# Decode attention over a long cache: jumps back announced in all passes but the last, and a new order of the closing work

## The chip, the cores and the metric

One core of a Trainium2 chip. Its engines work side by side (their busy shares are in the table below): PE multiplies matrices, DVE and ACT work on vectors, SP starts the transfers, which 16 DMA engines carry. The metric is the device time of one execution in microseconds, median of several. A profile was taken of one execution of each kernel; its span is about 2 us shorter than the time of the same execution (2523.2 of 2525.35 us before).

## The reference, cut to what matters

```python
x = A_x; xn = _layernorm(x)                       # 1 x 1 x 448
q = (xn @ wq).reshape(1, 1, 16, 256)              # 16 heads, Dh = 256
scores = einsum("bhqd,bhkd->bhqk", q, k_cache) * Dh**-0.5     # 65536 keys per head
o = einsum("bhqk,bhkd->bhqd", softmax(scores), v_cache)
s = o.reshape(1, 1, 4096) @ wo
g = _silu(_silu(xn @ w1) @ w2)
return x + s * g
```

K and V caches are 537 MB each in bf16. Everything else is small.

## The kernel before: the parts that matter here

The caches are cut into 64 blocks of 8 MB for each of K and V (block i, counted from 0: head i // 4, a quarter of the keys). Three buffers `R[0..2]` of 8 MB take K block i, whose products with the query are summed by DVE (19 of 32 columns) and ACT (13 of 32), and then V block i, which PE multiplies with the exponentials. SP starts the loads. Each engine has its own loop of three blocks a pass, DVE and ACT with 21 passes and PE with 20; the rest is written out behind the loops.

```python
def load_k(i, s): take(sp, vf[s]); sp.dma_start(out=R[s], in_=block(Kd, i)).then_inc(kl[s], 16); ...
def load_v(i, s): take(sp, kf[s]); sp.dma_start(out=R[s], in_=block(Vd, i)).then_inc(vl[s], 16)

def pe_block(i, s):
    pe_turn()       # turn (transpose) O, the result of an earlier block: 8 small products
    pe_max(i)       # transpose row maxima, next query, broadcast the maximum
    pe_v(s)         # 64 products 128x512 with a V block; then vf[s] is free

def loop(e, a, b, step, **kw):
    return nc.Fori(a, b, step, engines={e}, head_slot={e: 0}, **kw)

with loop(ET.DVE, 0, LAST - 2, NR, hint_back_edge=True) as i: ...          # LAST = 63, NR = 3
with loop(ET.Activation, 0, LAST - 2, NR, hint_back_edge=True) as i: ...
with loop(ET.PE, 1, LAST - 4, NR, hint_back_edge=True) as i: ...
pe_block(NBLK - 3, 0)     # block 61: its PE work includes the products with V block 60
pe_turn(); pe_v(1)        # V block 61
pe_max(NBLK - 2)
...
# SP: K 63 in two halves once V 60 is used (vf[0]); V 62 in 4 parts; V 63 keys 0..64 in 2 parts;
#     first 2 parts of wo; V 63 keys 64..128 in 4 parts; last 2 parts of wo
# PE, closing:
keys(psO, 2, 2, vn, nl, 0, 3, True); pe_rows()                 # V 62
keys(psO, 2, 2, vn, nl, 3, 4, False, od); pe_bcast()
...
keys(psO2, 0, 1, vz, zl, 0, 2, True, od); pe_turn()            # V 63, keys 0..64
project(*pieces[0]); pe_rows(); project(h0, h0 + 3); pe_bcast(); project(h0 + 3, h1)
t15 = pe_sums(...)
keys(psO, 0, 1, vz, zl, 2, 3, True); pe_turn()                 # keys 64..96
keys(psO, 0, 1, vz, zl, 3, len(vz), False, od)                 # keys 96..128
project(*pieces[2]); pe_turn(); project(...)                   # the end
```

`hint_back_edge=True` puts, at the head of every pass, an instruction that announces the jump back at the end of the pass.

## Time and profile before

| what | before | how to read it |
|---|---|---|
| time | 2526.43 us (2525.76 to 2526.54, 3 runs) | median and range |
| span of the profiled run | 2523.2 us | its time was 2525.35 |
| busy: DVE, ACT, PE | 89%, 57%, 47% | shares of the span |
| DMA queue that loads the caches | 99.5% of 16 engines' span | the limit |
| from the row maxima of block 61 to the end | 104.6 us | see below |

The last line is a measure I use throughout: from the start of DVE's row-maximum reduction for K block 61 (2418.61 us, about where the loops end) to the end of the span. I call it the **closing stretch**. It is good to 0.1 us, as the span is printed. (The texts before the experiments call that block 62, counted from one.)

### The profile page before, as it was taken

What the parts mean: (1) busy time and instruction counts of PE and PEld (TensorE: products, weight loads), DVE (VectorE), ACT (ScalarE), POOL (GpSimd) and SP (SyncE); (2) the same over time, 40 slices, a digit from 0 to 9 for tenths busy, and PEclk for the clock granted to TensorE, in tenths of its full rate; (3) what the DMA queues carried; (4) which work ended last, traced back from release to release, by engine and by line L of the source; (5) the groups of instructions that cost most, each with busy time, mean ns of one, the idle gap of its engine ahead of it and who ended that gap; (6) DMA issues with size and microseconds to landing.
All of it is one profiled execution on the core that took longest, in us unless ns stands there. A gap on an engine that the chain in (4) does not pass through costs nothing. (4 is left out here: it accounts for less than half of the span.)

```text
span 2523.2 us, 29918 instructions
## 1 busy us (share of the span) xinstructions
PE 1198.1 (47%) x5125; PEld 500.5 (20%) x5125; DVE 2233.7 (89%) x10281; ACT 1443.9 (57%) x6992; POOL 2.5 (0%) x13
## 2 busy tenths in 40 slices
PE   3353543534535435445354354454553543534556
PEld 2121211212212112112121121221221211212222
DVE  6989889889899898898898988988989889889886
ACT  3656556556555565565565655655656556556554
POOL 0000000000000000000000000000000000000000
PEclk7676767767767767677676676676766767767778
DMA  9999999999999999999999999999999999999998
GB/s 423 417 430 433 434 431 433 433 432 432 432 432 432 433 434 437 434 435 433 433 433 432 432 432 432 432 433 434 439 434 433 433 433 433 432 432 432 432 412 346
DMA packets 22728, 1084.52 MB, mean 430 GB/s; under 512 B 2354, under 2 KB 4532, under 8 KB 4916
## 3 DMA queue, kind: packets, MB, share of 16 engines
q1 hardware_dynamic: 22706, 1084.30, 99.5%
q8 instruction: 6, 0.10, 0.0%
q14 instruction: 14, 0.11, 0.0%
q10 hardware_dynamic: 2, 0.00, 0.0%
HBM read 1084.29 MB, written 0.00 MB: 430 GB/s over the span
## 5 line engine op out<-in xcount | busy, mean ns | idle before, releaser
L271 ACT ACTIVATE R<-R 128x256 bf16<-128x256 bf16 x3328 | 1330.7, 401 | 697.1 <-ACTq L154 697.1
L249 DVE CUSTOM_DVE_ANT_0 R<-R,qcur 128x256 bf16<-128x256 bf16 x4864 | 1700.2, 417 | 0.0
L318 PE MATMUL bank<-R,PV 128*2 128x512 bf16 x4096 | 1023.7, 416 | 32.4 <-DMA R<-in_A_v_cache_dram 15.3
L238 DVE TENSOR_TENSOR R<-R,qcur 128x3328 bf16<-128x3328 bf16 x256 | 482.6, 1885 | 198.7 <-DVEq L154 198.6
L271 ACT ACTIVATION_READ_ACCUMULATOR R<-R 128x1 f32 x3328 | 620.2, 186 | 2.6 <-issue 2.6
L330 PE MATMUL bank<-ident,rmax 128*1 128x128 bf16 x65 | 17.1, 263 | 1021.6 <-PEq L154 1021.6
L318 PEld LDWEIGHTS bank<-R,PV 128*2 128x2 bf16 x4096 | 365.0, 90 | 663.1 <-issue 208.0
L249 DVE DVE_READ_ACCUMULATOR2_ANT S<- 128x1 f32 x4864 | 383.5, 79 | 0.0
L346 PE MATMUL bank<-eye,O 2*128 2x1 f32 x536 | 98.0, 300 | 236.8 <-PEq L154 236.8
L330 PEld LDWEIGHTS bank<-ident,rmax 128*1 128x1 bf16 x65 | 5.2, 79 | 1026.1 <-issue 1025.9
L346 PEld LDWEIGHTS bank<-eye,O 2*128 2x128 f32 x536 | 94.2, 257 | 254.8 <-issue 254.8
L284 ACT ACTIVATE hist<-bank 128x1 f32 (+1 forms) x65 | 11.1, 171 | 203.4 <-ACTq L154 203.4
L305 ACT COPY hist<-bank 128x2 f32 (+1 forms) x66 | 10.5, 160 | 120.0 <-ACTq L154 120.0
L214 DVE TENSOR_REDUCE gmax<-bank 1x1 bf16<-1x128 f32 x65 | 18.2, 281 | 36.2 <-DVEq L154 36.2
L231 DVE CAST qcur<-bank 128x256 bf16<-128x256 f32 x64 | 27.2, 425 | 20.2 <-DVEq L154 18.3
L297 ACT COPY O<-bank 2x512 f32<-2x512 f32 x67 | 37.5, 559 | 9.1 <-ACTq L154 9.1
L286 ACT ACTIVATE PV<-S,hist 128x128 bf16<-128x128 f32 (+1 forms) x65 | 26.0, 400 | 13.4 <-ACTq L154 13.1
L358 PE MATMUL bank<-q,ident 16*128 16x256 bf16 x63 | 24.4, 387 | 0.0
L224 DVE COPY S<-S 128x128 f32<-128x128 f32 (+1 forms) x65 | 14.7, 226 | 9.5
L225 DVE TENSOR_REDUCE rmax<-S 128x1 bf16<-128x128 f32 (+1 forms) x65 | 18.2, 279 | 0.0
L336 PE MATMUL bank<-gmax,ones_row 1*128 1x1 bf16 x65 | 10.3, 158 | 15.9 <-PEq L154 15.9
L336 PEld LDWEIGHTS bank<-gmax,ones_row 1*128 1x128 bf16 x65 | 6.5, 99 | 33.3 <-issue 33.3
(65 smaller groups left out, 101.7 us busy)
## 6 DMA issues: line engine op xcount, KB each, us to landing
R<-in_A_k_cache_dram SPq DMA_DIRECT2D x4, 4096.0 KB, 23.4
R<-in_A_v_cache_dram SPq DMA_DIRECT2D x7, 2048.0 KB, 23.1
R<-in_A_wq_dram SPq DMA_DIRECT2D x1, 3072.0 KB, 12.7
R<-in_A_wo_dram SPq DMA_DIRECT2D x2, 1120.0 KB, 17.5
R<-in_B_w_dram SPq DMA_DIRECT2D x1, 1568.0 KB, 27.2
R<-in_B_w_dram SPq DMA_DIRECT2D x1, 1344.0 KB, 5.8
R<-in_A_v_cache_dram SPq DMA_DIRECT2D x1, 1024.0 KB, 15.8
R<-in_A_v_cache_dram SPq DMA_DIRECT2D x2, 512.0 KB, 17.0
```

The costliest lines, as they stand in the source:

```text
L214: dve.reduce_max(out=gmax[0:1, :], in_=ps_m[0:1, :], axis=AX.X).then_inc(gm, 1)
L225: dve.reduce_max(out=rmax[:, :], in_=S[:, c0:c1], axis=AX.X).then_inc(rm, 1)
L231: dve.tensor_copy(out=qcur[:, :], in_=ps_q).then_inc(sd, 1)
L238: m = dve.tensor_tensor(out=pair, in0=pair, in1=qcur[:, None, :].to_broadcast([P, NA, Dh]), op=ALU.mult,)
L249: ins = dve.tensor_tensor_reduce(out=Kv[:, c, :], in0=Kv[:, c, :], in1=qcur[:, :], scale=1.0, scalar=0.0, op0=ALU.mult, op1=ALU.add, accum ...
L271: ins = act.activation(out=prod, in_=prod, func=ACT.Identity, accum_out=S[:, c : c + 1],)
L286: act.activation(out=PV[s][:, c0:c1], in_=S2[:, c0:c1], func=ACT.Exp, bias=col(0, 1), scale=scale, accum_out=col(1, 2),).then_inc(pv, 1)
L297: act.copy(out=O[:, :], in_=po).then_inc(oc, 1)
L318: ins = pe.matmul(po, lhsT=PV[t][:, c : c + 2], rhs=R[s][:, c * Dh : (c + 2) * Dh], start=(start and c == k0), stop=(stop and c == k1 - 2),)
L330: pe.matmul(ps_m[0:1, :], lhsT=rmax[:, 0:1], rhs=ident[:, :], start=True, stop=True).then_inc(tm, 1)
L346: ins = pe.matmul(ps_t[:, a : a + 1], lhsT=Ov[:, j, a, :], rhs=eye2[:, j : j + 1], start=(j == 0), stop=(j == 1),)
L358: pe.matmul(ps_q, lhsT=ident[0:H, at(h)].to_broadcast([H, P]), rhs=q16[:, :], start=True, stop=True,).then_inc(qr, 1)
```

## The change

Its intent: let the engines leave their loops without a stall, and use the time won by an order of the closing work in which the row maxima are turned early and the last V block comes in smaller parts.

```diff
-    def loop(e, a, b, step, **kw):
-        return nc.Fori(a, b, step, engines={e}, head_slot={e: 0}, **kw)
+    @contextmanager
+    def loop(g, a, b, step):                       # (set-up of register, names, alignment cut)
+        with nc.body(head, valid_engines=es):
+            g.br_eq(r, b - step, on_true=body, on_false=ann)      # last pass: announce nothing
+        with nc.body(ann, valid_engines=es):
+            hint = g.mark_branch_hint_location()
+            nc.br(body, engines=es)
+        with nc.body(body, valid_engines=es):
+            yield nc.snap(r, min_val=a, max_val=b - step)
+            nc.regs_alu(r, r, step, op=mybir.AluOpType.add)
+            g.br_lt(r, b, on_true=head, on_false=tail).branch_hint(hint)
-    vz = cuts(0, 32, 64, 96, 112, 120, 128)
+    vz = cuts(0, 32, 64, 80, 96, 112, 120, 128)
-        keys(psO, 2, 2, vn, nl, 0, 3, True)
+        keys(psO, 2, 2, vn, nl, 0, 2, True)
         pe_rows()
-        keys(psO, 2, 2, vn, nl, 3, 4, False, od)
+        keys(psO, 2, 2, vn, nl, 2, 3, False)
         pe_bcast()
+        keys(psO, 2, 2, vn, nl, 3, 4, False, od)
 ...
-        keys(psO2, 0, 1, vz, zl, 0, 2, True, od)
+        keys(psO2, 0, 1, vz, zl, 0, 1, True)
         pe_turn()
+        pe_rows()
+        keys(psO2, 0, 1, vz, zl, 1, 2, False, od)
+        pe_bcast()
         project(*pieces[0])
-        pe_rows(); project(h0, h0 + 3); pe_bcast(); project(h0 + 3, h1)
         t15 = pe_sums(ps_m[:, 0:NL], N1, NENT)
-        keys(psO, 0, 1, vz, zl, 2, 3, True)
         pe_turn()
-        keys(psO, 0, 1, vz, zl, 3, len(vz), False, od)
-        project(*pieces[2])
+        project(*pieces[1])
+        keys(psO, 0, 1, vz, zl, 2, len(vz), True, od)
+        project(h0, h0 + 2)
         t = pe_turn(tok=True)
+        project(h0 + 2, h1)
```

(Waits, ACT's and DVE's lines and moves within a line are cut.)

## The prediction

> **What bounds the kernel now.** I read the page first, then the chain that ended last, then stretches of the end, then the time order of single engines. The page's slices and its queue table say that the transfers are the limit for nearly all of the span:

> ```profile
> span 2523.2 us, 29918 instructions
> DMA  9999999999999999999999999999999999999998
> GB/s 423 417 430 433 434 431 433 433 432 432 432 432 432 433 434 437 434 435 433 433 433 432 432 432 432 432 433 434 439 434 433 433 433 433 432 432 432 432 412 346
> q1 hardware_dynamic: 22706, 1084.30, 99.5%
> ```

> The reader is to see 432 to 434 GB/s in slice after slice, and less only in the first two and the last two. One slice is 63 us. 1084.30 MB at 432.5 GB/s take 2507 us of the 2523: at most 16 us can be had without moving fewer bytes, and they sit at the ends. So this change, which moves no bytes, can gain only single microseconds of 2526, and the verdict of a 2% test (50 us) is all but settled. What is worth predicting is where those few microseconds go.

> The table of stretches near the end shows one hole in the stream (the last two columns are the DMA share and GB/s):

> ```profile
> 2380.00:2420.00 40.00, 19.94 (x79) 8.24 (x79) 35.40 (x163) 22.46 (x109) 0.00 (x0) 0.67 1.02 441
> 2420.00:2440.00 20.00, 14.31 (x55) 4.96 (x55) 16.73 (x78) 11.26 (x55) 0.00 (x0) 0.72 0.99 424
> 2440.00:2460.00 20.00, 18.34 (x91) 7.86 (x89) 17.75 (x83) 11.71 (x56) 0.00 (x0) 1.00 0.84 348
> ```

> PE in order of time shows its cause: three products of the first V block after PE's loop, then a stall, then the other 61.

> ```profile
> 2420.18 1.44 PE L318 MATMUL bank<-R,PV 128*2 128x512 bf16 x3
> 2427.17 15.35 PE L318 MATMUL bank<-R,PV 128*2 128x512 bf16 x61 [5.55 <-issue]
> 2442.35 0.17 PE L368 MATMUL bank<-ident 128*1 128x1 bf16 x1
> ```

> "issue" means that nothing in the profile held the engine: it had no instruction. The last K block may be loaded only when that V block has been used, so its load leaves SP at 2442.65, when the queue has run dry. DVE shows the same at its own exit: the query is in PSUM at 2458.62, the copy of it starts 7 us later.

> ```profile
> 2458.56 0.28 DVE L214 TENSOR_REDUCE gmax<-bank 1x1 bf16<-1x128 f32 x1 [0.94 <-DVEq L154]
> 2465.61 0.42 DVE L231 CAST qcur<-bank 128x256 bf16<-128x256 f32 x1 [6.77 <-DVEq L154]
> ```

> The DMA records of the trace agree: between 109 and 2424 us there is no instruction fetch at all, then a 16 KB one starts at 2424.64 (PE goes on at 2427.17) and an 8 KB one at 2463.76 (DVE goes on at 2465.61). In the last 16 us PE is the bound, without a pause:

> ```profile
> 2507.47 3.61 PE L318 MATMUL bank<-R,PV 128*2 128x512 bf16 x16 [0.99 <-DMA R<-in_A_v_cache_dram]
> 2511.01 1.10 PE L346 MATMUL bank<-eye,O 2*128 2x1 f32 x8
> 2512.04 3.61 PE L318 MATMUL bank<-R,PV 128*2 128x512 bf16 x16
> 2515.49 1.68 PE L662 MATMUL bank<-R,OT 128*1 128x448 bf16 x8
> 2517.10 1.10 PE L346 MATMUL bank<-eye,O 2*128 2x1 f32 x8
> 2518.13 1.01 PE L662 MATMUL bank<-R,OT 128*1 128x448 bf16 x4
> ```

> [...]a jump was announced and not taken. [...]granted clock 0.66 in 2460 to 2480, which holds a 9 us wait of PE, and 1.00 where it is busy.

> **The change part by part.** *The loops.* They run the same passes (21, 21 and 20) of the same bodies. Each pass gets a compare-and-branch and two short jumps: [...]none of it on the path, since the DVE has 11% of the span idle. In the last pass nothing is announced, so the block behind the loop should be fetched in time. That removes 5.55 us from PE and about 6.8 us from DVE.

> What PE's part is worth: V blocks in mid-loop take 15.3 to 16.4 us, so this one would end near 2436.5, not 2442.35, and the load of the last K block would leave 6 us earlier, before the queue is dry. The hole, 348 instead of 432 GB/s over 20 us, is (432-348)/432 x 20 = 3.9 us; by the byte records of 2436 to 2446 alone 2.7 us. But a transfer has landed only with its slowest DMA engine. In the landing records the last block before the hole reaches most of the 16 engines at 2441.6 to 2442.1, the laggard at 2443.5, and the hole lets the laggard catch up. So later landings come 0 to 2.7 us earlier; I take 1.3.

> What DVE's part is worth: its last block starts near 2458.8 instead of 2465.61. PE idles before the V block that precedes it and begins it with a cold clock, so I give back 0.5 us: 6.3 us earlier. The second half's row maxima, which PE turns at 2503.67 now, are then ready at about 2497.3.

> *The closing order.* From there PE is the path in the new order, with durations by start-to-start from the rows above: 16 products 3.45, a turn 1.03, a product of the projection 0.2. From 2497.3: row maxima 0.05; V keys 32 to 64, 3.45 (2500.8); broadcast 0.1; ten projection products 2.0 (2502.9); sums 0.36 (2503.3); turn 1.03 (2504.3); ten projection products 2.0 (2506.3); 32 products for keys 64 to 128, 6.9 (2513.2); four of the projection 0.8 (2514.0); turn 1.03 (2515.0); the last eight with the DVE's step behind them 1.8 (2516.8). After PE's last product the kernel now needs 2523.2 - 2519.14 = 4.06 us (two DVE operations and the store): 2520.9.

> Transfers needed on that way, by the landing records of before: V keys to 96 at 2507.4, to 112 at 2510.0, to 120 at 2511.3, to 128 at 2512.6, third part of wo at 2514.75, fourth at 2515.9. Less 1.3 each they are just in time, but for the third part of wo: 2513.45 against 2513.2. That adds 0.3. Splitting keys 64 to 96 in two lets PE begin before the whole has landed; it saves a wait, no work. Sum: 2521.2, with 0.1 for rounding 2521.3, which is 1.9 us less than 2523.2. Timed: 2526.4 - 1.9 = **2524.5 us**.

> **The rivals.** (1) *The hint is not what stalls the exits, or the fetch still comes late.* Then the DVE's maxima stay at 2503.7, and the new order, in which PE waits for them before V keys 32 to 64, is a bad one: everything after shifts by over 6 us, to a time near 2531. For it: the new loop is spread over four code blocks with jumps, none ever seen here. Against: three records (stall, fetch, restart) match at both exits. (2) *The laggard keeps its lag.* Transfers end no earlier, the third part of wo is waited for until 2514.75, and 1.3 us of the gain is lost: 2525.8. For it: the last landings spread over 3 us from the first to the last DMA engine. (3) *The whole hole is won and PE does not wait*: 2.7 us off the landings, 2523.9 by the sum above, because PE's work and not the transfers then ends last; 2522 if the row maxima come earlier too. (4) *The hint fails in every pass*: stalls of 6 us, 20 times. DVE's slack, about 3.9 us per block of 39, would hide most, yet up to 40 us could show. The mid-span rate would drop below 432.

> **Range and chances.** Rivals 2 and 3 span 2522 to 2526; rival 1 I hold at one in ten, rival 4 at one in fifty. Runs of before lie within 0.8 us. So 2522.3 to 2526.6 for eight in ten. Faster by over 2% is excluded by the bytes (0.2%); slower by over 2% would need more than rival 4 (0.8%); 99% within.

> **What would show it right or wrong.** Right: no "issue" pause among PE's V products near 2420; instruction fetches before 2420; the load of the last K block leaving SP near 2437; 420 to 435 GB/s in 2440 to 2460; the query's copy near 2459; the row maxima's product near 2497; PE without long pauses from there; its last product near 2517. Wrong: an "issue" pause or a 6 us wait still there at an exit; a wait of the final projection for wo of over 1 us; any fall of the mid-span rate; a new pause on PE where it waits for the row maxima.

The cost of the new loop's branches was an estimate that no trace here times, and it was left out of the sum. That an announced jump which is not taken makes the engine stall at the exit was an assumption then; E2 and E7 tested it. Why PE paused for 5.55 us when its fetch, at 2424.64, took 1.07 is not shown.

The figures from the trace of the kernel before: PE's wait ended with the last DMA engine: V keys 64 to 96 landed from 2504.18 (first engine) to 2507.43 (last), and PE began with them at 2507.47. Over the hole the last engine's lag behind the first fell from 2.02 us (block landed at 2443.57) to 0.39 (at 2454.65). The clock: V block 61 took 13.97 us, all of it at a granted clock of 1.00; the block before it began at 0.50. The 0.5 us given back for the cold start was a guess.

## The result and the profile after

The changed kernel: 2529.76 us median of 4 runs (2525.78, 2529.27, 2530.25, 2530.26), the kernel before in the same rounds 2526.1 (2524.6 to 2526.54). The ratio is 1.0012 with a 95% interval of 0.9995 to 1.0029: the same. A ratio is the mean time of one kernel's fast runs over that of the other's of the same rounds, so not quite the ratio of the medians. With later runs (E1, E11, E12) there are 11 of the changed kernel: 2525.78 to 2530.26, median 2527.78. The 40 of the kernel before in all rounds reach from 2524.4 to 2529.4, with medians of 2526.1 to 2526.65 in each set. So the change shows no gain, where I had forecast 1.9 us. By the medians of all runs it costs about 1 us, which is not clear of noise.

The profiled run took 2525.78 us. The page of the changed kernel, its span and rate lines:

```profile
span 2523.9 us, 29978 instructions
GB/s 423 403 432 438 437 433 435 433 432 432 432 432 432 432 436 435 435 435 435 432 432 432 432 432 432 432 436 436 434 437 433 432 432 432 432 432 432 433 431 326
```

Mid-span is unchanged at 432 GB/s. The last slice but one is now 431 where it was 412: the hole is gone. The stretches around it, in the changed kernel (last two columns: DMA share and GB/s):

```profile
2420.00:2440.00 20.00, 17.25 (x67) 6.09 (x66) 16.68 (x75) 11.55 (x56) 0.00 (x0) 0.83 1.00 431
2440.00:2460.00 20.00, 17.82 (x76) 7.73 (x76) 18.30 (x87) 10.91 (x54) 0.00 (x0) 0.83 0.97 415
```

PE in order of time, changed kernel: no "issue" pause any more, but the second V block shown, 61, is slower than before.

```profile
2420.75 16.89 PE L318 MATMUL bank<-R,PV 128*2 128x512 bf16 x64
2437.48 0.17 PE L368 MATMUL bank<-ident 128*1 128x1 bf16 x1
2443.62 15.71 PE L318 MATMUL bank<-R,PV 128*2 128x512 bf16 x64 [1.50 <-PEq L154]
```

The same V block (61) in the kernel before:

```profile
2444.35 13.97 PE L318 MATMUL bank<-R,PV 128*2 128x512 bf16 x64
```

DVE at its exit, changed kernel: the wait before the query's copy is 0.87 us in place of 6.77, and the copy starts at 2460.71 in place of 2465.61.

```profile
2459.56 0.28 DVE L214 TENSOR_REDUCE gmax<-bank 1x1 bf16<-1x128 f32 x1 [1.39 <-DVEq L154]
2460.71 0.42 DVE L231 CAST qcur<-bank 128x256 bf16<-128x256 f32 x1 [0.87 <-DVEq L154]
```

The end on PE, changed kernel:

```profile
2498.78 0.26 PE L330 MATMUL bank<-ident,rmax 128*1 128x128 bf16 x1 [4.83 <-PEq L154]
2498.84 5.08 PE L318 MATMUL bank<-R,PV 128*2 128x512 bf16 x16
2503.84 0.17 PE L336 MATMUL bank<-gmax,ones_row 1*128 1x1 bf16 x1
...
2509.16 7.07 PE L318 MATMUL bank<-R,PV 128*2 128x512 bf16 x32
2516.07 0.92 PE L681 MATMUL bank<-R,OT 128*1 128x448 bf16 x4
2517.07 1.07 PE L346 MATMUL bank<-eye,O 2*128 2x1 f32 x8
2518.07 1.68 PE L681 MATMUL bank<-R,OT 128*1 128x448 bf16 x8
```

PE waits 4.83 us for the last row maxima, and the 16 products behind that wait, whose V keys had landed at 2494.2 by the trace's landing records, take 5.08 us; elsewhere 16 of them take 3.61. The stretches of the changed kernel there show why (the last column but two is the granted clock):

```profile
2489.00:2493.00 4.00, 3.69 (x18) 1.41 (x18) 4.00 (x16) 1.39 (x8) 0.00 (x0) 1.00 0.95 370
2493.00:2498.70 5.70, 0.95 (x8) 0.86 (x8) 5.49 (x32) 4.04 (x22) 0.00 (x0) 0.67 1.06 400
2498.70:2502.00 3.30, 3.22 (x9) 1.06 (x10) 0.28 (x1) 0.00 (x0) 0.00 (x0) 0.53 1.02 424
```

The landing records say what the loops won: V 63's last part landed at 2510.2 (before: 2512.6), the third part of wo at 2512.4 (2514.75), the fourth at 2513.55 (2515.9). Transfers end 2.3 us earlier, and the kernel does not: its closing stretch is 104.7 us, before 104.6. The experiments ask where the 2.3 us went, and why three of the first four runs are longer still.

### The profile page after: what moved, and what is told of

Read it like the earlier page. It is cut to its first block, busy times and chain, and to the rows that moved or that the text cites. A ratio compares the mean times of both kernels' runs of the same rounds, so it can differ in the third digit from the quotient of the medians.

```text
span 2523.9 us, 29978 instructions
## 1 busy us (share of the span) xinstructions
PE 1205.0 (48%) x5125; PEld 502.8 (20%) x5125; DVE 2233.4 (88%) x10281; ACT 1443.7 (57%) x6992; POOL 2.5 (0%) x13
## 3 DMA queue, kind: packets, MB, share of 16 engines
q1 hardware_dynamic: 22850, 1084.30, 99.5%
## 5 line engine op out<-in xcount | busy, mean ns | idle before, releaser
L318 PE MATMUL bank<-R,PV 128*2 128x512 bf16 x4096 | 1031.3, 419 | 22.3 <-DMA R<-in_A_v_cache_dram 9.2
L318 PEld LDWEIGHTS bank<-R,PV 128*2 128x2 bf16 x4096 | 367.0, 90 | 658.5 <-issue 215.3
L249 DVE DVE_READ_ACCUMULATOR2_ANT S<- 128x1 f32 x4864 | 378.0, 78 | 0.0
L346 PE MATMUL bank<-eye,O 2*128 2x1 f32 x536 | 98.6, 301 | 236.8 <-PEq L154 236.7
L346 PEld LDWEIGHTS bank<-eye,O 2*128 2x128 f32 x536 | 94.8, 259 | 254.4 <-issue 254.3
L214 DVE TENSOR_REDUCE gmax<-bank 1x1 bf16<-1x128 f32 x65 | 18.3, 281 | 36.7 <-DVEq L154 36.7
L231 DVE CAST qcur<-bank 128x256 bf16<-128x256 f32 x64 | 27.2, 425 | 16.4 <-DVEq L154 14.7
## 6 DMA issues: line engine op xcount, KB each, us to landing
R<-in_A_v_cache_dram SPq DMA_DIRECT2D x2, 512.0 KB, 16.3
```

Of the source, the lines that this page charges most:

```text
L214: dve.reduce_max(out=gmax[0:1, :], in_=ps_m[0:1, :], axis=AX.X).then_inc(gm, 1)
L231: dve.tensor_copy(out=qcur[:, :], in_=ps_q).then_inc(sd, 1)
L249: ins = dve.tensor_tensor_reduce(out=Kv[:, c, :], in0=Kv[:, c, :], in1=qcur[:, :], scale=1.0, scalar=0.0, op0=ALU.mult, op1=ALU.add, accum ...
L318: ins = pe.matmul(po, lhsT=PV[t][:, c : c + 2], rhs=R[s][:, c * Dh : (c + 2) * Dh], start=(start and c == k0), stop=(stop and c == k1 - 2),)
L346: ins = pe.matmul(ps_t[:, a : a + 1], lhsT=Ov[:, j, a, :], rhs=eye2[:, j : j + 1], start=(j == 0), stop=(j == 1),)
```

## The experiments

**Theory.** The loops do what they are for and win 2 to 3 us; the closing order gives it back, since it lets PE stand still until the DVE's last row maxima, with 16 products behind the wait whose data are there, and with a clock that has fallen. **Rivals:** the new loops bring a cost of their own; or the transfers end last whatever PE does. A second question is why three of the first four times lie 4 us above the fourth.

| run | what | median us (range, runs) | ratio to before [95%] | closing stretch |
|---|---|---|---|---|
| first | the change | 2529.76 (2525.78 to 2530.26, 4) | 1.0012 [0.9995, 1.0029] | 104.7 |
| E1 | the change again | 2526.87 (2525.82 to 2530.12, 5) | 1.0004 [0.9991, 1.0018] | 104.7 |
| E2 | loops only | 2523.43 (2522.72 to 2527.51, 5) | 0.9990 [0.9976, 1.0004] | 102.3 |
| E3 | closing order only | 2531.67 (2531.32 to 2535.31, 5) | 1.0023 [1.0010, 1.0037] | 110.8 |
| E4 | change, keys first | 2524.02 (2522.35 to 2527.45, 5) | 0.9996 [0.9982, 1.0009] | 101.1 |
| E5 | change, warm start | 2527.57 (2526.95 to 2529.45, 5) | 1.0004 [0.9990, 1.0017] | 105.8 |
| E6 | change, idle products in the wait | 2527.26 (2524.82 to 2527.76, 5) | 0.9998 [0.9985, 1.0012] | 105.6 |
| E7 | before, nothing announced | 2626.84 (2626.22 to 2628.15, 4) | 1.0397 [1.0381, 1.0413] | 103.9 |
| E8 | before, new loop on PE alone | 2528.22 (2526.58 to 2529.24, 5) | 1.0005 [0.9991, 1.0019] | 105.4 |
| E9 | keys first, tuned | 2522.15 (2521.67 to 2524.07, 5) | 0.9985 [0.9971, 0.9998] | 100.6 |
| E10 | before, new loop on DVE alone | 2527.83 (2526.26 to 2528.56, 4) | 1.0005 [0.9990, 1.0021] | 105.7 |
| E11, E12 | the change, one look each | 2526.82; 2527.78 | none | 105.6; 104.6 |
| E13 | change, plain loop on PE | 2527.76 (2527.35 to 2530.71, 5) | 1.0007 [0.9993, 1.0021] | 107.0 |
| E14 | E9, plain loop on PE | 2523.47 (2521.95 to 2524.72, 5) | 0.9988 [0.9974, 1.0002] | 101.2 |

The closing stretch is of the one traced run of each.

**E1: the changed kernel again.** No edit.

> The changed kernel once more, unchanged, because three of its four runs took 2529.3 to 2530.3 us and the profiled one 2525.8. Theory A (two timings of one program: something that varies from run to run, an instruction fetch or the phase of PE's clock, delays the closing work in most runs): times again fall in two groups near 2525.8 and 2530, and a trace of the long group shows the extra 4.4 us after 2420 us, as a pause or as slow products. Rival B (an accident of one chip): all runs near 2525.8.

Measured: 2525.8, 2526.4, 2526.9, 2528.2 and 2530.1 us (on chip 9; the record does not name the chip of the first set). So the spread came again, but it is no clean pair of groups. The traced run (2526.39) has the closing stretch of the first, 104.7.

**E2 and E3: each half of the change alone.** E2 is the kernel before with the new `loop` and its three calls. E3 is the changed kernel with the old loops:

```diff
-        with loop(pe, 1, LAST - 2, NR) as i:          # and the same for dve and act
+        with loop(ET.PE, 1, LAST - 4, NR, hint_back_edge=True) as i:
```

> The kernel before with only the new loops. Theory A (the loops remove the exit stalls, and the landings of the last transfers come 2.3 us earlier as in the changed kernel's trace; the closing order is what gives it back): 1.5 to 3 us faster than before, 2523.5 to 2525, PE without an issue pause near 2420 and the row maxima's product of the last half near 2498.5. Rival B (the new loops themselves bring the long runs): as slow as the changed kernel in part of its runs, 2529 to 2530.

> The kernel before with only the new closing order, with the old loops and their stalls. Theory A (in the new order PE stands still until the DVE's last row maxima, and works cold after it): the maxima's product stays near 2503.7, everything behind it shifts, 2530 to 2532, that is 4 to 6 us slower than before. Rival B (the order is harmless, the loops are to blame): within 1 us of before.

In time both came out as the theory has it. Three of E2's five runs took 2522.7 to 2523.4, two 2527.0 and 2527.5 (its interval against before still reaches 1.0004); no issue pause; the closing stretch is 102.3, 2.3 us less. One detail was missed: I expected the product of the last row maxima near 2498.5, and it came at 2506.51. This trace arrived 4 us late, and 16 products behind a wait of 2.40 us, which took 5.30 us (3.61 in the kernel before, at a granted clock of 1.00), came before it. E3 is 5 us slower than before. PE in E3 shows the wrong wait at its full length:

```profile
2503.16 0.26 PE L330 MATMUL bank<-ident,rmax 128*1 128x128 bf16 x1 [8.34 <-PEq L154]
2503.22 6.36 PE L318 MATMUL bank<-R,PV 128*2 128x512 bf16 x16
```

The order costs 6.2 us with the old loops (110.8 - 104.6) and 2.4 with the new (104.7 - 102.3). It is a loss both times; the loops pay for it. The order does have the maxima earlier: DVE starts them 79.2 us into the closing stretch in the changed kernel, 81.0 in E2. What PE does around its wait for them costs more than that wins.

**E4: the keys before the row maxima.**

```diff
         pe_turn()
-        pe_rows()
         keys(psO2, 0, 1, vz, zl, 1, 2, False, od)
-        pe_bcast(); act_softmax(LAST + 1, 0, HK, KB); act_out(psO2)
+        pe_rows()
         project(*pieces[0])
+        pe_bcast(); act_softmax(LAST + 1, 0, HK, KB); act_out(psO2)
```

(Lines joined, waits cut.)

> The changed kernel with one thing put back: the product of the last row maxima comes after the V keys 32 to 64 and not before them, and ten projection products run while the DVE takes the maximum. Theory A (the wait for the row maxima is in the wrong place: it holds back 16 products whose data landed at 2494.2 until 2498.8 and lets PE's clock fall, 5.08 us for 3.5): 3 to 5 us faster than the changed kernel's runs of the same rounds, 2521.5 to 2523, faster than before. Rival B (transfers end last anyway): at most 1 us faster than the changed kernel.

Measured: 2522.35, 2523.87 and 2524.02 in three runs, 2526.8 and 2527.45 in two. The median is 2.9 us below that of the changed kernel in the same rounds, a little less than I expected, and not clear of the kernel before. In its trace the 16 products run as soon as their keys land, in 3.61 us, while the DVE still works:

```profile
2494.50 3.61 PE L318 MATMUL bank<-R,PV 128*2 128x512 bf16 x16 [0.26 <-DMA R<-in_A_v_cache_dram]
2499.02 0.22 PE L330 MATMUL bank<-ident,rmax 128*1 128x128 bf16 x1 [0.90 <-PEq L154]
2499.18 2.05 PE L681 MATMUL bank<-R,OT 128*1 128x448 bf16 x10
```

The row maxima come no earlier than in the changed kernel (2499.02 against 2498.78), and the closing stretch is 101.1 in place of 104.7. So 3.6 us of the changed kernel's closing work is due to this one place (the edit also puts ten projection products into the DVE's next step, so the share of the keys alone is not separated). "Transfers end last" would have allowed 1 us at most and is out.

**E6: idle products in that wait.** The wrong order kept, 18 products of constants put before `pe_rows()`.

> The changed kernel with 18 idle products in PE's wait for the last row maxima, so that its clock stays up. Theory A (that wait costs twice, the wait itself and the slow clock after it): the 16 products after it take 3.5 us, not 5.1 to 5.2, and the end comes 1.6 us earlier than the changed kernel's, 2524.2 in its short group. Rival B (transfers end last): no gain. The long group, if it comes from the start, stays, 4 us above.

A miss as a test. In the traced run, one of the longer ones, the idle products ended 3.2 us too early and the 16 products were slow again (5.30 us for 3.61):

```profile
2493.26 4.08 PE L603 MATMUL bank<-ident 128*2 128x512 bf16 x18
2500.50 0.22 PE L330 MATMUL bank<-ident,rmax 128*1 128x128 bf16 x1 [3.17 <-PEq L154]
2500.55 5.30 PE L318 MATMUL bank<-R,PV 128*2 128x512 bf16 x16
```

So what the slow clock alone costs was not tested; 1.5 us is an estimate from the durations, 5.08 in the changed kernel (granted clock 0.53 from 2498.7 to 2502) against 3.61 in E4.

**E8 and E10: the new loop on one engine.** The kernel before with the new loop on PE alone (E8) or on DVE alone (E10).

> The kernel before with the new loop on PE alone. Theory A (PE's exit is what held the last K block's load, and with it all later transfers): the load leaves near 2437, the hole near 2441 is closed, landings come 1.3 to 2.3 us earlier, but the DVE still starts its last block near 2465.5, so the last row maxima stay at 2503.5 and half or more of the gain is lost: within 1 us of before. Rival B (DVE's exit doesn't matter in the old closing order): as fast as the kernel with all new loops, 2522.7 to 2523.4 in its short group.

> The kernel before with the new loop on DVE alone. Theory A (in the old closing order DVE's exit stall is hidden by the late transfers; PE's exit is what delays those): the query's copy near 2459.5, the last K block's load still near 2442.5, the hole still there, the stretch from block 62's row maxima to the end 103.5 to 104.6 us against 104.6 before: no faster than before, 2524.5 to 2526.5. Rival B (DVE's exit is what counts): 102.3 us, as with all new loops.

Neither gains. In E8 the last K block's load leaves at 2438.1 and the hole is closed, but the DVE still waits 6.27 us at its exit, and the row maxima of the last half come at 2506.2. In E10 the DVE is in time (2459.93), but PE still pauses for 5.85 us and the load leaves at 2442.87. Both stretches are 0.8 to 1.1 us longer than before, about what single traces differ by; E10's was expected at 103.5 to 104.6. Both traces hold 16 products of 5.2 to 5.6 us, behind waits of PE of 1.6 to 4.7 us. The 2.3 us of E2 need both exits: with one alone, neither the time nor the closing stretch gets shorter.

**E7: nothing announced.** `hint_back_edge=True` removed in all three loops.

> The kernel before without any announcement of the jumps back. Theory A (an armed announcement is what keeps the block behind the loop from being fetched): no stall at the exits of PE and DVE, the last K block's load leaves near 2437 plus any delay, but fetches in every pass[...], stalls of some us per pass there, most of it in their slack: 2524 to 2560. Rival B (exits stall for the fetch whatever was announced): 5 to 7 us stalls at the exits as before.

The page of E7, its rate and its fetches on the queue that had 14 packets before:

```profile
GB/s 422 403 432 424 416 413 416 422 403 426 407 415 419 413 418 413 416 417 415 412 420 414 418 411 408 427 402 421 411 418 415 416 414 420 412 418 415 416 419 328
...
q14 instruction: 114, 0.93, 0.1%
```

Its exits: PE's first V block behind its loop in one piece, and DVE's copy of the query with no wait before it.

```profile
2522.58 15.87 PE L318 MATMUL bank<-R,PV 128*2 128x512 bf16 x64
...
2563.20 0.42 DVE L231 CAST qcur<-bank 128x256 bf16<-128x256 f32 x1
```

100 us slower, far over the 2560 us that I had set as the most: the DVE waits 132.6 us in 21 places for the copy of the query, 6.3 us a pass, where it goes back to its loop's head. At the exits of PE and DVE there is no stall (5.55 and 6.77 us before), with no new loop at all. So in these runs it is the announcement that makes the exit stall, and on DVE its absence that makes the jump back stall. For DVE, announcing in all passes but the last is right. PE is the exception: even here there are only 6 fetches of 16 KB in all (q8, as before), so its loop needs no announcement.

**E5: a warm start.** PE's first pass written out, with 70 idle products ahead of the first V block.

> The changed kernel with PE's first pass written out and 70 idle products before the first V block, so that it starts with a full clock. In the trace of the long run (kernel with the new loops alone) the delay of 3.7 us was there by 330 us: the first load that has to wait for PE left at 117.9, after the stream had run dry, and one DMA engine was a 64 KB packet behind from then on. Theory A (the long runs come from that hole at the start): the first V block takes 14 us and not 16.3, its load leaves near 115 with the stream still full, all times come 1 to 2.4 us earlier and the group near 2530 is gone: 2523.5 to 2525 in all runs. Rival B (the long runs come from elsewhere): both groups stay, each perhaps 1 us earlier.

The first V block took 13.97 us and its load left at 115.13, as wanted, and the second slice moved 416 GB/s, not 403. But all five runs are between 2526.95 and 2529.45: the long runs did not go away. That does not clear the hole at the start, since the edit seems to have brought a delay of its own. With the first pass written out, the trace has fetches of 16 KB at 182.42 and 192.09 us that the changed kernel's lacks. The block that landed at 178.5 was on time (178.34 in the changed kernel); the next landed at 198.86, 1.1 us late, with two engines 0.9 us behind the rest, and the loads run late from there on.

**E11 and E12: the changed kernel.**

> The changed kernel unchanged, one look, to catch a run of its long group (near 2530) with a trace. Theory A (the closing work always takes 104.7 us and the long runs arrive 4 us later at it): the row maxima of block 62 at 2423 and 104.7 us from there. Rival B (the closing work itself takes longer in the long runs): arrival near 2419.5 and 108 us or more from there. If it falls in the short group it only counts as one more run.

> The same as the look before it, once more, for a second chance at a trace of the long group: Theory A 104.7 us from the row maxima of block 62 to the end whatever the total; Rival B 108 us or more in a run near 2530.

No run near 2530 was caught. E12, at 2527.78, has 104.6 us from the row maxima to the end and those maxima at 2421.32 in place of 2419.18: what made it 2 us longer lay before the closing work. The same in E2's trace, a run of 2527.05: the maxima at 2422.68. There the rate shows where, in the slices from 126 to 378 us:

```profile
GB/s 422 402 429 432 427 425 436 433 433 439 434 433 432 432 432 432 433 433 433 440 435 434 432 432 432 432 433 432 434 439 436 433 433 432 432 432 432 432 431 343
```

By its landing records one of the 16 engines was 2.2 us behind all others by 142 us (E5's text calls it a packet of 64 KB; the median of those took 2.42 us in the kernel before, from 1000 to 2000 us); after that the loads were issued late (the next V block's at 176.3, 173.9 in the changed kernel). Why one engine falls behind in some runs stays open.

**E13 and E14: a plain loop on PE.** What E1 to E12 left open is that the changed kernel also arrives later at the closing work. In the traces with the new loop on PE the last V load in one piece (block 61; "second to last" in the texts) leaves later. SP before:

```profile
2380.13 0.33 SPq L197 DMA_DIRECT2D R<-in_A_v_cache_dram  x1
...
2418.84 0.33 SPq L197 DMA_DIRECT2D R<-in_A_v_cache_dram  x1
```

and in the changed kernel:

```profile
2379.99 0.33 SPq L197 DMA_DIRECT2D R<-in_A_v_cache_dram  x1
...
2419.41 0.33 SPq L197 DMA_DIRECT2D R<-in_A_v_cache_dram  x1
2437.77 0.82 SPq L201 DMA_DIRECT2D R<-in_A_k_cache_dram  x2
```

The interval is 38.71 us before, and 38.7 in E3 and E10; it is 39.42 here, and 39.0 to 40.1 in all ten traces with the new loop on PE, 39.6 on average. The landing records tell why: from 2325 on the first and the last of the 16 DMA engines land each block at a fixed distance, 0.84 us in the changed kernel. At 2351.7 PE fetches the 16 KB behind its loop, 1.07 us on one engine, and from the next block on the distance is 1.47 us, up to the end of the loops.

```diff
-        with loop(pe, 1, LAST - 2, NR) as i:
+        with nc.Fori(1, LAST - 4, NR, engines={ET.PE}, head_slot={ET.PE: 0}) as i:
```

> The changed kernel with a plain loop on PE, without any announcement; DVE and ACT keep the new loop. In all ten traces with the new loop on PE the slowest DMA engine falls back by 0.6 to 1.4 us when PE fetches 16 KB near 2350, and the second to last V load leaves 39.0 to 40.2 us after the one before it; in the three traces with the old loop on PE it is 38.7. In the kernel without announcements PE fetched once, at 141 us, and never again before its exit. Theory A (that late fetch is what makes the new loop arrive later at the closing work): the fetch moves to about 141, the interval is 38.7, no stall at PE's exit, the closing stretch stays 104.6 to 105.6, and the time falls by about 1 us against the changed kernel, 2524.5 to 2527. Rival B (the interval comes from the new loop's extra instructions, or the plain PE loop stalls): 39 us or more still, or pauses of PE in the loop.

> The tuned kernel with the same plain loop on PE. Theory A: interval 38.7, closing stretch near 100.6, times 1 us below the tuned one's, 2520.5 to 2522 in its short group and the long group as rare as in the kernel before. Rival B: as the tuned one, 2521.7 to 2524.1.

(The text on record has the jump of the distance in all ten traces. In E2's it stayed, 1.23 to 1.24 us: the engine that had been first took the fetch and became the last. The interval, 39.02, was long all the same.)

The interval is 38.7 in both, PE's fetch is at 143 us in E13, and there is no stall at its exit: the cause of the late interval is shown. Nor is a fetch's delay always kept: after E14's at 141 us the distance rose from 1.58 to 2.31 us and was back at 1.37 by 450 us. The times did not follow: E13's are as long as the changed kernel's, E14's as E9's or longer. E13's traced closing stretch is 107.0, because V block 61 there took 16.87 us (15.71 in the changed kernel, 13.97 before) and PE waited 7.42 us for the maxima. So the fetch explains the interval; that it makes the runs longer is not shown.

**E9: a version that beats both.** E4, with 18 idle products around PE's waits ahead of V block 61, and projection products moved into PE's pauses:

```diff
         pe_block(NBLK - 3, 0)
+        warm(10)
         pe_turn()
+        warm(8)
         pe_v(1)
 ...
         keys(psO2, 0, 1, vz, zl, 1, 2, False, od)
+        project(h0, h0 + 1)
         pe_rows()
-        project(*pieces[0])
+        project(h0 + 1, h1)
         pe_bcast()
+        project(*pieces[1])
         t15 = pe_sums(ps_m[:, 0:NL], N1, NENT); pe_turn()
-        project(*pieces[1])
         keys(psO, 0, 1, vz, zl, 2, len(vz), True, od)
-        project(h0, h0 + 2); t = pe_turn(tok=True); project(h0 + 2, h1)
+        t = pe_turn(tok=True); project(*pieces[2])
```

(Lines joined, waits cut.)

> The kernel with the keys first (the version that did best so far), with idle products that keep PE's clock up before the second to last V block, and with the projection's products moved into PE's two remaining pauses. From the row maxima of block 62 on DVE to the end the changed kernel needs 104.7 us by its trace, the keys-first one 101.1. Theory A (PE's own work decides this stretch): 13.97 us, not 15.5 to 16.6, for that V block and pauses filled: 99.5 to 100.5 us, 2521 to 2522 in the short group. Rival B (the last transfers decide: fourth part of wo at 2513.85 and the tail after it): no better than 101.

2522.15 us against 2526.61 of the kernel before in the same rounds, ratio 0.9985, interval below 1. It is the only version clearly faster than before, and its five runs (2521.67 to 2524.07) lie below all 11 of the changed kernel. Its closing stretch is 100.6, half a microsecond less than E4's, which is within what single traces differ by, and not the 99.5 to 100.5 that I had hoped for. PE, in E9:

```profile
2444.70 14.40 PE L318 MATMUL bank<-R,PV 128*2 128x512 bf16 x64
...
2489.59 5.30 PE L318 MATMUL bank<-R,PV 128*2 128x512 bf16 x16 [2.25 <-DMA R<-in_A_v_cache_dram]
2494.82 1.10 PE L346 MATMUL bank<-eye,O 2*128 2x1 f32 x8
2495.85 3.61 PE L318 MATMUL bank<-R,PV 128*2 128x512 bf16 x16
```

The idle products made V block 61 shorter (14.40 us in place of 15.71), but it began 1.1 us later, behind them. And after a wait of only 2.25 us for V keys 0 to 32 the granted clock was 0.57 from 2489.6 to 2492 (1.00 from 2487 to 2489.6), 16 products took 5.30 us, and the next 16 started at 2495.85 although their keys had landed at 2494.49.

## Why the prediction was wrong, step by step

In short: the step that failed is the cost of the 16 products behind the wait for the row maxima, and before it the time of those maxima. Together they made the traced run 2.6 us longer than the sum. What made most runs longer than the traced one is only partly known.

- **What bounds the kernel, and that the verdict is "the same":** right. No byte was moved less and mid-span stayed near 432 GB/s (the slices before range from 430 to 439, not from 432 to 434).
- **The exits stall because of the announcement; the new loop ends it:** right, and shown by E2 and E7. PE's pause of 5.55 us is gone; of DVE's 6.77 us a wait of 0.87 is left, which the prediction did not have.
- **The hole closes and landings come 0 to 2.7 us earlier, 1.3 taken:** right in kind, 2.3 measured; 1.3 was a guess within a range. Rival 1, that the exit stall stays, did not happen. Of rival 2 half did: the last engine kept its lag behind the first (3.4 us at the last landing, 3.1 before), but all landings came earlier, so its loss of 1.3 us did not follow.
- **Row maxima at about 2497.3:** measured 2498.78, 1.5 us late. Two terms were mis-sized. I gave back 0.5 us for the cold start of V block 61; that block took 15.71 us for 13.97 (the granted clock was 0.50 until 2447.16) and the query was ready 1.0 us later than before, at 2459.62. And DVE's wait of 0.87 us was missing.
- **"V keys 32 to 64, 3.45 (2500.8)":** the step that failed. They took 5.0 us to the next product, 1.55 more. The prediction itself put PE into a wait for the maxima just before them, and itself set the granted clock of 0.66 beside a 9 us wait of PE, but took its durations from rows of the kernel before, in which PE had been busy. After that step the sum holds to 0.15 us: projection, turn and 32 products began 2.9 us late (2509.16 against 2506.3) and the last product ended 2.95 us late (2519.75 against 2516.8).
- **The order's worth.** I added up its work from the maxima on and never asked what the old order would make of the new loops. E2 answers: 102.3 against 104.7. What rival 1 says of late maxima, that the order is then a bad one, held here although the exit stalls were gone and the maxima came 1.5 us late and not 6. (E3, which is rival 1's case, took 2531.67 us; the forecast for it was near 2531.)
- **From trace to time.** The prediction has 2521.3 for the span; 2523.9 was measured in a short run, whose time, 2525.78, lies inside my range. That is the 2.6 us of the steps above. The median of the first four runs was another 4 us longer. I took the spread before (0.8 us in three runs) for the kernel's, so my range was too narrow; the spread is 5 us in 40 runs, and the changed kernel's runs lay in the long part more often. A delay of the first 330 us shows in E2 (3.7 us), E12 (1.8) and, with fetches of its own, E5. PE's late fetch may add to it (0.3 to 1.4 us by the intervals), but without it (E13) the times were no shorter. Why the first set had three of four runs near 2530 was not caught in a trace and stays open.
- **Slips in the text.** Rival 3's 2523.9 does not follow from the sum, which gives 2524.1 to 2524.2. Rival 4's "up to 40 us" was too low: E7, with such a stall of DVE in every pass, cost 100. And the 9 us wait before 2470.98, beside which I set the granted clock of 0.66, is not shown to have caused it: the clock records have 0.50 from 2462.02, 0.1 us into the wait, to 2475.67.

## What to carry to other kernels

When a change moves products behind a wait, time them with the clock that they will have behind that wait, not with that of the row they come from (16 products: 5.08 us for 3.61 in the changed kernel), and put behind a wait only what needs it. Announce a loop's jump back on an engine that would otherwise fetch in every pass (DVE here, 6.3 us a pass in E7), and not in the last pass (6.77 us at DVE's exit before, 0.87 after); on an engine that would not (PE here, 6 fetches in all in E7), leave it out, though E13 and E14 show no time won by that. Look at instruction fetches beside a full stream of transfers: near the end of the loops, one of 1.07 us put off the last landing of every block until the loops ended, by 0.6 us in the changed kernel.
